# Weight splits moved from GpSimd to VectorE in a routing stage, and the first expert's second weights loaded during it

## The chip, the cores and the metric

One core of one Trainium2 chip runs the whole kernel. The time is device microseconds of one execution. The engines are named as in the profile: PE (TensorE, matmuls; its weight loads are PEld), DVE (VectorE), ACT (ScalarE), POOL (GpSimd) and SP (SyncE, which here only issues transfers). Each engine works through its own instructions in order; semaphores hold an instruction until what it needs is there, and everything queued behind it on that engine waits too.

## The reference

Attention over 4 x 12 heads of 448 tokens, then a mixture of 8 experts with a fixed capacity of 224 tokens each, then a two-layer feed-forward net. Cut to what matters:

```python
x = attention(q, k, v)                       # 1792 tokens x 768
logits = x @ w_gate                          # 1792 x 8
for idx in argsort(-logits.flatten()):       # best (token, expert) pair first
    tok, e = idx // 8, idx % 8
    if assigned[tok] < 0 and counts[e] < 224:
        assigned[tok] = e; counts[e] += 1
for e in range(8):
    out[assigned == e] = relu(x[assigned == e] @ w1[e]) @ w2[e]
h = out @ w_in                               # 768 -> 2048
result = elu(h) @ w_out                      # 2048 -> 768
```

## The kernel before

**Stages.** Attention (to about 302 us), routing (to about 336), the experts (to about 590), the two layers of the last net (to the end). Products are made in float16 pairs: each float32 operand becomes a high half (ACT, a rounding copy) and a low half (what is left: operand times scale minus the high half), and a product is three matmuls (high x high, high x low, low x high).

**Routing** (`Route.run`, L562). Attention leaves the logits `L`. A first round and four more (`round_`, L626; `KSTEP` is 5) raise a price per expert: POOL multiplies (`V`, L628), DVE picks each token's best expert (`choose`) and then in `raises` computes `s` (L602), `u` (L606) and a comparison `gd` (L612); PE counts tokens per expert over the 128 partitions (`cnt`, L617 and L619), DVE tests the count (`ind`, L620), PE turns that into the step, DVE applies it to `U` (L634). It is one chain through DVE and PE; PE fills its waits with nine 512-wide matmuls on constants per round (`warm`). `place` (L639) turns the choice into positions (`pre`, on PE), a 0/1 matrix `Pm` and the token index list `idx` (matmuls `ip`). Then POOL gathers the rows of expert 0 (`gather`, L857), and all engines load a flag `fi` and branch over a rare fallback (L700).

**Weights in the routing stage** (`Weights`, L758). Expert 0's `w1` comes in eight blocks of 128x768. Five float32 stage buffers hold them (`fa`); a buffer is free for the next load when its split is done. In each of the first four rounds ACT scales a block in place (`W.scale`, L773) and later makes its high half (`W.high`, L779), and POOL makes the low half in the next round (`W.low`, L785). The last four blocks get high halves behind the last round and low halves on DVE behind the branch (L926).

**Experts** (`moe`). `columns(e)` splits the gathered rows (`xg`) into halves `xh` (high on ACT L896; low on DVE for expert 0, on POOL L897 for the others) and transposes them on PE (`xt`, L904). The first products (`ph`, L940, 8 of 18 matmuls, three PSUM banks) end in a ReLU on ACT (L941) and a low half on DVE (L944), which together free the bank. The second products (`py`, L956) are 6 of 24 matmuls. `W.split` (L791, L800, L802) loads and splits the weights of all later experts; SP issues the loads. What stands inside `tc.manual_schedule()` is written in the order in which it is to be issued; everything else is placed by a scheduler that models time, and it may place its instructions between those of a manual block. The list `idx` is also stored to memory element by element (`lin`, L929, on ACT's queue) and read back on SP's (`id2`, L931) for the last scatter.

Of the kernel before, what the change touches and what calls it, by code (L numbers as in the profile page):

```python
# [504 lines left out]
class Route:  # L505
# [54 lines left out]
    def run(self, L, idx, row_d, W, gather):  # L560
# [9 lines left out]
        with tc.tile_pool(name="rt", bufs=1, reuse_waits="tile") as sp, \  # L570
# [55 lines left out]
            def round_(n, Lc, r, *beside):  # L626

                nc.gpsimd.tensor_tensor(V, U, bc(r), ALU.mult)  # L628
                W.low()
# [6 lines left out]
                if beside:  # L636
                    W.high()

            def place():  # L639
# [13 lines left out]
                Pm, Q = T("Pm", [P, 112, NT], F16), T("Qm", [P, NT, 2, 8], F16)  # L653
                nc.gpsimd.tensor_tensor(Q[:, :, 0], oh, self.tok.unsqueeze(2).broadcast_to(tile3), ALU.mult)
# [13 lines left out]
                nc.vector.tensor_copy(fi, f)  # L668

# [16 lines left out]
            with tc.manual_schedule():  # L686
                for h in H:
                    nc.vector.tensor_tensor(U[:, h], L[:, h], bc(self.t0, h.stop - h.start), ALU.subtract)
                warm(8)
                round_(0, L, self.iw, W.scale, relative)  # L690
                for k in range(1, KSTEP):
                    round_(1, Ln, self.r, *(W.scale,) * (k < KSTEP - 1))
                for k in range(4, 8):
                    W.high(False)
                choose(Ln)
                fi = place()
                gather()
                warm(3)
# [59 lines left out]
class Weights:  # L758

    def __init__(self, tc, ring, w1_d):  # L760
        self.tc, self.nc, self.wstage, self.ring = tc, tc.nc, ring, ring
        self.w1_d, self.fs, self.ws, self.todo = w1_d, [], [], None
# [7 lines left out]
    def scale(self):  # L770

        f = self.fs[len(self.ws)]
        self.nc.scalar.activation(f, f, AF.Copy, scale=SW)  # L773

    def high(self, scaled=True):
# [3 lines left out]
        self.nc.scalar.activation(w[:, 0], f, AF.Copy, scale=1.0 if scaled else SW)  # L779
        self.todo = f, w  # L780

    def low(self):
        if self.todo:
            f, w = self.todo
            self.nc.gpsimd.tensor_tensor(w[:, 1], f, w[:, 0], ALU.subtract)  # L785
            self.todo = None
            self.load()
# [6 lines left out]
    def split(self, tag, bufs, src, n, name, f=None):  # L794
        nc = self.nc
        if f is None:
            f = self.stage(src, n, name)
# [63 lines left out]
def moe(tc, xs, idx, idh, W, rows, ring, w1_d, w2_d, wi_d, wo_d, lin, g_d, t_d, out):  # L861
    nc = tc.nc
    with tc.tile_pool(name="xc", bufs=1, reuse_waits="tile") as xp, tc.tile_pool(name="mp", bufs=1, space=PSUM, reuse_waits="tile") as pp:
# [19 lines left out]
        with tc.tile_pool(name="m1", bufs=1, reuse_waits="tile") as sp:  # L883
# [34 lines left out]
            with tc.manual_schedule():  # L918
# [4 lines left out]

                nc.vector.tensor_copy(ix2[0:112], idx[0:112])
                for f in range(4, 8):
                    nc.vector.scalar_tensor_tensor(W.ws[f][:, 1], W.fs[f], SW, W.ws[f][:, 0], ALU.mult, ALU.subtract)  # L926
                W.after = columns(0)
# [3 lines left out]
            nc.sync.dma_start(id2, lin.rearrange("(g p) -> p g", p=P))  # L931
            for e in range(E):
                x = xe[e]
                h = sp.tile([P, 8, 2, CAP], F16, tag="h", name=f"h{e}", bufs=2)
                for f in range(8):
                    w = W.ws[f] if e == 0 else W.split("w1", 8, w1_d[e, f], 768, f"w1_{e}_{f}")
# [5 lines left out]
                    if e == 0 and f == 3:  # L942
                        W.after = relu.ins
                    nc.vector.scalar_tensor_tensor(h[:, f, 1], ps, 0.0, h[:, f, 0], ALU.max, ALU.subtract)  # L944
# [6 lines left out]
                for d in range(6):  # L951
                    w = W.split("w2", 6, w2_d[e, d], 1024, f"w2_{e}_{d}", W.fs[8 + d] if e == 0 and d < 4 else None)
# [4 lines left out]
                    result(e, d, ps)  # L957
        with tc.tile_pool(name="wb", bufs=1, reuse_waits="tile") as wp:
# [176 lines left out]
```

## Time and profile before

| | |
|---|---|
| Median of three runs | 1012.69 us (1010.31 to 1017.13) |
| Profiled execution | 1012.46 us, of it span 1010.7 |
| PE busy | 956.9 us, 95% |
| DVE busy | 757.9 us, 75% |
| ACT busy | 525.1 us, 52% |
| POOL busy | 292.6 us, 29% |
| Chain that ended last | PE 54%, DMA 8%, DVE 2% |

A row of a timeline has the start in us, the length in us, the engine, the line, the operation, what it writes and reads, and how many instructions were merged (x18); in brackets the engine's idle time before it and what ended that. A row of a group by line has the busy sum and the mean of one, then the idle time before the group and who ended it. In a row of a tile are the shortest, median and longest duration in ns. The chain of waits is the path that ended last, in order of time.

### The profile page before, as it was taken

The numbers are of one execution on the slowest core, as the hardware profiler recorded it, in microseconds if no ns is written. First come the engines' busy times: TensorE is split into PE (matmuls) and PEld (weight loads), VectorE is DVE, ScalarE is ACT, GpSimd is POOL, SyncE is SP. The second block draws the span as 40 slices with busy tenths as digits, with TensorE's granted clock in tenths as the row PEclk, the third lists the DMA queues.
The fourth block names the chain that finished last, engine by engine and source line by source line (L and its number), as shares of the span: only waits on it lengthen the run. The fifth ranks groups of instructions, "written<-read, shape, count | busy, mean of one in ns | idle before, by whom it ended". The sixth has DMA issues, their size and how long they took to land.

```text
span 1010.7 us, 18583 instructions
## 1 busy us (share of the span) xinstructions
PE 956.9 (95%) x6922; PEld 630.2 (62%) x6922; DVE 757.9 (75%) x1412; ACT 525.1 (52%) x1152; POOL 292.6 (29%) x438
## 2 busy tenths in 40 slices
PE   5899999999997878999999999999999989999997
PEld 2445555555554568999999965555555546666664
DVE  7899999999958458877778699999933574555530
ACT  4778888888864256666664443343411333332330
POOL 5678888888623530221100000000000001000000
PEclk7999999999998889999999999999999999999999
DMA  9434344344221589977777258788784653333100
GB/s 343 150 104 127 118 116 147 114 126 138 51 52 53 82 248 313 289 252 231 219 235 218 80 185 275 248 261 273 216 260 123 191 156 100 109 116 101 46 32 32
DMA packets 100639, 164.92 MB, mean 163 GB/s; under 512 B 32960, under 2 KB 66240, under 8 KB 100160
## 3 DMA queue, kind: packets, MB, share of 16 engines
q1 hardware_dynamic: 95760, 150.56, 47.4%
q0 software_dynamic: 2400, 11.01, 3.3%
q10 hardware_dynamic: 2384, 2.10, 1.3%
q8 instruction: 56, 0.92, 0.4%
q14 instruction: 39, 0.32, 0.1%
HBM read 131.66 MB, written 31.99 MB: 162 GB/s over the span
## 4 chain that ended last, share of the span: by engine, by line
PE 54%; DMA 8%; DVE 2%; issue 1%; ACT 0%; SPq 0%; POOL 0%; POOLq 0%; ACTq 0%; DVEq 0%
PE l L1034 17%; PE py L956 10%; PE o_b L1073 10%; PE ph L940 9%; PE o_c L1073 6%; DMA g_d<-e 3%; PE o_a L1073 2%; DMA fw<-w 2%; DMA xg<-xs,idx 1%; DMA q<-g_d 1%; PE xt L904 1%; DVE e L1038 0%; DMA out<-xc,id 0%; DVE w L802 0%; DVE e L1037 0%
## 5 line engine op out<-in xcount | busy, mean ns | idle before, releaser
L1034 PE MATMUL l<-xc,wic 128*128 128x384 f16 (+1 forms) x1152 | 218.2, 352 | 0.0
L1034 PEld LDWEIGHTS <-wic 128*128 128x128 f16 x1152 | 112.7, 98 | 104.8
L1073 PEld LDWEIGHTS <-a 128*128 128x128 f16 x1080 | 106.1, 98 | 75.2 <-ACT a L1010 3.5
L1089 POOL DMA_INDIRECT out<-xc,id x14 | 14.4, 1030 | 468.8 <-DVE xc L1082 443.1
L802 DVE SCALAR_TENSOR_TENSOR w<-fw,w 128x768 f16<-128x768 f32 (+1 forms) x100 | 114.9, 1154 | 27.9 <-ACT w L800 27.6
L244 ACT ACTIVATE p<-s,nb,r 128x448 f32<-128x448 f32 x144 | 103.9, 722 | 31.2 <-DVE nb L231 30.9
L956 PE MATMUL py<-h,w 128*128 128x224 f16 x1152 | 113.8, 259 | 2.0 <-ACT h L941 1.2
L956 PEld LDWEIGHTS <-w 128*128 128x128 f16 x1152 | 109.9, 98 | 2.6 <-issue 2.3
L225 DVE TENSOR_REDUCE nm<-s 128x1 f32<-128x448 f32 x168 | 102.9, 613 | 3.5 <-PE s L220 3.1
L940 PE MATMUL ph<-xe,w 128*128 128x224 f16 x1008 | 99.5, 259 | 2.5 <-DVE h L944 2.5
L800 ACT ACTIVATE w<-fw 128x768 f16<-128x768 f32 (+1 forms) x100 | 92.9, 932 | 15.2 <-DMA fw<-w 14.6
L940 PEld LDWEIGHTS <-w 128*128 128x128 f16 x1008 | 96.4, 98 | 3.1 <-issue 2.8
L1036 ACT ACTIVATE e<-l 128x512 f32<-128x512 f32 (+1 forms) x64 | 34.6, 540 | 113.0 <-PE l L1034 112.7
L297 PE MATMUL o<-e,v 128*64 128x448 f32 x384 | 87.8, 558 | 1.6 <-DVE xl L309 1.6
L282 ACT ACTIVATE e<-pt 128x448 f32<-128x448 f32 (+2 forms) x216 | 82.8, 422 | 12.3 <-PE pt L273 11.2
L273 PE MATMUL pt<-idn,p 128*128 128x128 f32 x432 | 71.2, 277 | 2.0 <-ACT p L244 1.5
L273 PEld LDWEIGHTS pt<-idn,p 128*128 128x128 f32 x432 | 50.4, 141 | 24.3 <-ACT e L282 16.7
L897 POOL TENSOR_TENSOR xh<-xg,xh 112x768 f16<-112x768 f32 x14 | 25.0, 1802 | 137.8 <-ACT xh L896 137.8
L220 PE MATMUL s<-ks,qh 128*128 128x448 f16 x144 | 52.0, 361 | 12.5 <-ACT p L244 10.8
L231 DVE TENSOR_TENSOR nb<-nm,r 128x1 f32<-128x1 f32 x168 | 59.4, 354 | 2.9
L1010 ACT ACTIVATE a<-s 128x1024 f16<-128x1024 f32 (+2 forms) x30 | 28.5, 966 | 55.4 <-PE o_b L1073 31.9
L1073 PE MATMUL o_b<-wb,a 128*128 128x384 f16 x312 | 52.7, 326 | 0.0
(246 smaller groups left out, 1653.8 us busy)
## 6 DMA issues: line engine op xcount, KB each, us to landing
fw<-w SPq DMA_DIRECT2D x44, 512.0 KB, 4.8
fw<-w SPq DMA_DIRECT2D x56, 384.0 KB, 3.9
xwi<-wi SPq DMA_DIRECT2D x16, 768.0 KB, 6.6
xwo<-wo SPq DMA_DIRECT2D x16, 768.0 KB, 4.9
q<-g_d SPq DMA_DIRECT2D x24, 512.0 KB, 3.7
qT<-qT SPq DMA_DIRECT2D x24, 448.0 KB, 4.1
qk<-qk SPq DMA_DIRECT2D x23, 448.0 KB, 3.4
g_d<-e SPq DMA_DIRECT2D x32, 256.0 KB, 4.4
```

The costliest lines, as they stand in the source:

```text
L225: nc.vector.tensor_reduce(d["nm", u], d["s", u][:, 0:448], AX.X, ALU.max, negate=True)
L231: nc.vector.tensor_tensor(d["nb", u], d["nm", u], d["r"][:, rc:rc + 1], ALU.mult)
L244: nc.scalar.activation(dst, d["s", u][:, 0:448], AF.Exp, bias=d["nb", u], scale=d["r"][:, rc:rc + 1], accum_out=d["sm"][:, rc:rc + 1])
L273: nc.tensor.transpose(pt[:, j * P:(j + 1) * P], p[j][:, h, 64 * h + c * P:64 * h + (c + 1) * P], idn)
L282: move = nc.vector.tensor_copy if u not in (0, 1, 2, 4, 5, 6) else lambda o, x: nc.scalar.activation(o, x, AF.Copy)
L297: nc.tensor.matmul(d["o"][64 * h:64 * h + 64, 0:448], d["v"][:, c + 4 * h, :], d["e", min(2 * c + h, 6)], start=c == 0, stop=c == 3)
L800: nc.scalar.activation(w[:, 0], f, AF.Copy, scale=SW)
L802: nc.vector.scalar_tensor_tensor(w[:, 1], f, SW, w[:, 0], ALU.mult, ALU.subtract)
L940: nc.tensor.matmul(ps, w[:, i, d * P:(d + 1) * P], x[:, d, j], start=d == 0 and n == 0, stop=d == 5 and n == 2)
L956: nc.tensor.matmul(ps, w[:, i, f * P:(f + 1) * P], h[:, f, j], start=f == 0 and n == 0, stop=f == 7 and n == 2)
L1034: nc.tensor.matmul(ps, w[:, i, d * P:(d + 1) * P], xc[cb][:, h, d, j], start=d == 0 and m == 0, stop=d == 5 and m == 2)
L1073: nc.tensor.matmul(ps, a[x][:, f, i], wt[b][f][:, j], start=first and f == 0 and k == 0, stop=f == 7 and k == 2, skip_group_check=True)
```

## The change

POOL makes no low halves any more. `W.scale` is gone: `W.high` makes the scaled high half inside `raises`, where `W.scale` stood, and `W.low` makes the low half on DVE in pieces of 384 columns: one piece in each of rounds 1 to 4 behind `gd`, two in `place` ahead of the product with `pre`, four ahead of the index list, six behind expert 0's gather. A pool for six blocks of `w2` (512 KB each) is opened before routing and loaded on SP's queue (`W.fetch`); two of their high halves are made behind the last round (`W.second`). Expert 0's first products stand inside the manual block, with the other halves of its `w2` between them (`W.second`, `W.rest`). The four `w2` loads that ACT issued before are gone. `idx` is copied for the store behind `columns(0)`.

```diff
             def round_(n, Lc, r, *beside):
                 nc.gpsimd.tensor_tensor(V, U, bc(r), ALU.mult)
-                W.low()
                 choose(Lc)
                 ...
-                if beside:
-                    W.high()
-            def place():
+            def place(first=lambda: None, second=lambda: None):
                 ...
+                first()
                 nc.gpsimd.tensor_tensor(Q[:, :, 0], oh, ...)
                 ...
                 nc.vector.tensor_copy(fi, f)
+                second()
                 ...
-                round_(0, L, self.iw, W.scale, relative)
+                round_(0, L, self.iw, W.high, relative)
                 for k in range(1, KSTEP):
-                    round_(1, Ln, self.r, *(W.scale,) * (k < KSTEP - 1))
-                for k in range(4, 8):
-                    W.high(False)
+                    round_(1, Ln, self.r, W.high, W.low)
                 choose(Ln)
-                fi = place()
+                fi = place(lambda: W.low(2), lambda: W.low(4))
                 gather()
+                W.second(2)
+                for k in range(3):
+                    W.high()
+                    W.low(2)
...
-    def low(self):
-        if self.todo:
-            f, w = self.todo
-            self.nc.gpsimd.tensor_tensor(w[:, 1], f, w[:, 0], ALU.subtract)
+    def low(self, n=1):
+        for _ in range(n):
+            k, h = divmod(self.halves, 2)
+            self.halves += 1
+            f, w, c = self.fs[k], self.ws[k], slice(384 * h, 384 * h + 384)
+            self.nc.vector.scalar_tensor_tensor(w[:, 1, c], f[:, c], SW, w[:, 0, c], ALU.mult, ALU.subtract)
+            if h:
+                self.load()
+    def fetch(self, pool, w2_d):
+        self.f2 = [pool.tile([P, 1024], F32, name=f"b{d}") for d in range(6)]
+        self.w2 = []
+        for f, x in zip(self.f2, w2_d[0]):
+            self.nc.sync.dma_start(f, x)
+    def second(self, n=1):
+        for _ in range(n):
+            d = len(self.w2)
+            w = self.ring.tile([P, 2, 1024], F16, tag="w2", name=f"w2_0_{d}", bufs=6)
+            self.w2.append(w)
+            self.nc.scalar.activation(w[:, 0], self.f2[d], AF.Copy, scale=SW)
+    def rest(self, d):
+        w = self.w2[d]
+        self.nc.vector.scalar_tensor_tensor(w[:, 1], self.f2[d], SW, w[:, 0], ALU.mult, ALU.subtract)
...
-                nc.vector.tensor_copy(ix2[0:112], idx[0:112])
-                for f in range(4, 8):
-                    nc.vector.scalar_tensor_tensor(W.ws[f][:, 1], W.fs[f], SW, W.ws[f][:, 0], ALU.mult, ALU.subtract)
                 W.after = columns(0)
+                nc.vector.tensor_copy(ix2[0:112], idx[0:112])
                 nc.scalar.dma_start(lin.rearrange("(h e r) -> r (h e)", h=2, e=E), ...)
-                W.fs += [W.stage(w2_d[0, d], 1024, f"b{d}", nc.scalar) for d in range(4)]
+                for f in range(8):
+                    relu = first(0, f, W.ws[f])
+                    if f == 3:
+                        W.after = relu.ins
+                    if f < 6:
+                        if f >= 2:
+                            W.second()
+                        W.rest(f)
             nc.sync.dma_start(id2, lin.rearrange("(g p) -> p g", p=P))
```

What this makes of the engines' orders, at the places that matter below. On DVE, in a routing round, from the comparison to the step; before:

```order
L612 TENSOR_TENSOR gd<-u,GG 128x128x4
L612 TENSOR_TENSOR gd<-u,GG 128x128x8
L620 TENSOR_SCALAR ind<-cnt,c_72 128x8
L634 TENSOR_TENSOR U<-V,k 128x48
L634 TENSOR_TENSOR U<-V,k 128x64
```

and after the change:

```order
L612 TENSOR_TENSOR gd<-u,GG 128x128x4
L612 TENSOR_TENSOR gd<-u,GG 128x128x8
L785 SCALAR_TENSOR_TENSOR wa_5076<-fa_4295,wa_5076 128x384
L620 TENSOR_SCALAR ind<-cnt,c_72 128x8
L633 TENSOR_TENSOR U<-V,k 128x48
L633 TENSOR_TENSOR U<-V,k 128x64
```

One half of a block has come between the comparison and the test that waits for PE's count.

On PE, behind the branch, inside expert 0's product 0 (`ph_0`, weights `wa`; `xt_0` with `xh_1` is a transpose of expert 1's halves); before, where products 0, 1 and 2 have had six matmuls each (`wa_5200` is product 2's weight):

```order
L940 LDWEIGHTS wa_5200
L940 MATMUL ph_2_6782<-xe_6683,wa_5200 128x224
L904 LDWEIGHTS xh_1_6914
L904 MATMUL xt_0_6919<-idh,xh_1_6914 128x112
L904 LDWEIGHTS xh_1_6914
L904 MATMUL xt_0_6919<-idh,xh_1_6914 128x112
L940 LDWEIGHTS wa_5086
L940 MATMUL ph_0_6740<-xe_6683,wa_5086 128x224
```

and after, where only product 0 has had six:

```order
L951 LDWEIGHTS wa_5076
L951 MATMUL ph_0_6752<-xe_6704,wa_5076 128x224
L922 LDWEIGHTS xh_1_6942
L922 MATMUL xt_0_6947<-idh,xh_1_6942 128x112
L922 LDWEIGHTS xh_1_6942
L922 MATMUL xt_0_6947<-idh,xh_1_6942 128x112
L951 LDWEIGHTS wa_5076
L951 MATMUL ph_0_6752<-xe_6704,wa_5076 128x224
```

Expert 1's transposes stand twelve matmuls earlier; the second of them needs the low half from POOL.

On ACT, behind the high halves of expert 0's columns (`xh` with `xg` of the two later experts, `lin` the index store, `fb` the `w2` loads, `h` the ReLUs, `w_1_5` a `w1` block of expert 1); before:

```order
L929 DMA lin<-ix_6646 112x16x1
L791 DMA fb_6729<-w 128x1024
L791 DMA fb_6731<-w 128x1024
L791 DMA fb_6733<-w 128x1024
L896 ACTIVATE xh_1_6914<-xg_1_6656 112x768
L791 DMA fb_6735<-w 128x1024
L896 ACTIVATE xh_0_6913<-xg_0_6655 112x768
L896 ACTIVATE xh_1_7348<-xg_1_6909 112x768
L941 ACTIVATE h_6739<-ph_0_6740 128x224
```

and after, the same place and, further on, that of the last ReLU:

```order
L914 ACTIVATE xh_1_6942<-xg_1_6682 112x768
L914 ACTIVATE xh_0_6941<-xg_0_6681 112x768
L914 ACTIVATE xh_1_7354<-xg_1_6937 112x768
L944 DMA lin<-ix_6672 112x16x1
L952 ACTIVATE h_6751<-ph_0_6752 128x224
...
L952 ACTIVATE h_6751<-ph_6_6892 128x224
L818 ACTIVATE w_1_5_7272<-fw_1_5_7270 128x768
L818 ACTIVATE w_1_6_7298<-fw_1_6_7296 128x768
L952 ACTIVATE h_6751<-ph_7_6913 128x224
```

The index store has gone behind the third gathered half, and two blocks of expert 1 stand ahead of the last ReLU. On SP the six `w2` loads stand behind attention's last stores, then the last three `w1` blocks, then (behind the flag's load, ahead of the branch) the first two `w1` blocks of expert 1; behind the branch three more, `id2`, and only then `w1` blocks 5 to 7.

## Rows read from the trace of the kernel before

**Rows 1.** Chain of waits, from 387 us (start, length, what)
```profile
387.36 0.45 PE ph L940 x3
...
447.23 13.80 PE ph L940 x144
```

**Rows 2.** Timeline of PE, expert 0's first products
```profile
345.41 1.89 PE L940 MATMUL ph<-xe,wa 128*128 128x224 f16 x18
...
359.13 8.89 PE L940 MATMUL ph<-xe,wa 128*128 128x224 f16 x72 [5.85 <-DVE h L944]
```

**Rows 3.** PE's groups by line, 342 to 388 us
```profile
L940 PE MATMUL ph<-xe,wa 128*128 128x224 f16 x144 | 16.2, 278 | 5.9 <-DVE h L944 5.9
L956 PE MATMUL py<-h,w 128*128 128x224 f16 x76 | 8.1, 259 | 2.0 <-ACT h L941 1.2 <-DVE h L944 0.8
L940 PE MATMUL ph<-xe,w 128*128 128x224 f16 x57 | 6.1, 259 | 2.3 <-DVE h L944 2.3
```

**Rows 4.** Timeline of ACT, high halves of gathered rows, first ReLUs
```profile
350.14 0.84 ACT L896 ACTIVATE xh<-xg 112x768 f16<-112x768 f32 x1 [4.96 <-DMA xg<-xs,idx]
357.56 0.84 ACT L896 ACTIVATE xh<-xg 112x768 f16<-112x768 f32 x1 [6.58 <-DMA xg<-xs,idx]
358.31 0.83 ACT L941 ACTIVATE h<-ph 128x224 f16<-128x224 f32 x3
```

**Rows 5.** Tile xg (gathered rows), 330 to 382 us
```profile
DMA to landing us min/median/max: 3.8/8.4/15.9
```

**Rows 6.** Timeline of DVE in routing, rounds 0, 1 and 2
```profile
303.47 0.34 DVE L602 SCALAR_TENSOR_TENSOR s<-V,oh 128x48 f32<-128x48 f32 x2
...
307.42 1.72 DVE L602 SCALAR_TENSOR_TENSOR s<-V,oh 128x48 f32<-128x48 f32 x2
...
311.11 0.23 DVE L620 TENSOR_SCALAR ind<-cnt,c 128x8 f16<-128x8 f32 x1 [0.74 <-PE cnt L619]
...
312.72 1.79 DVE L602 SCALAR_TENSOR_TENSOR s<-V,oh 128x48 f32<-128x48 f32 x2
```

**Rows 7.** Tile fa (w1 stage buffers), 300 to 392 us
```profile
L785 POOL TENSOR_TENSOR wa<-fa,wa x4: 1637/1639/1691, 307.2 to 323.4; 128x768 f16<-128x768 f32 x4
...
DMA to landing us min/median/max: 3.0/3.1/3.1
```

**Rows 8.** Timeline of DVE, the operation of the halves at two widths
```profile
237.64 0.62 DVE L309 SCALAR_TENSOR_TENSOR xl<-o,xh 128x448 f16<-128x448 f32 x1
...
402.11 0.38 DVE L944 SCALAR_TENSOR_TENSOR h<-ph,h 128x224 f16<-128x224 f32 x1
```

**Rows 9.** Stretch table (us, PE busy, granted clock, DMA share, GB/s)
```profile
302.00:328.00 26.00, 20.67 (x141) 0.87 0.19 56
...
388.00:420.00 32.00, 31.75 (x343) 1.00 0.92 308
```

**Rows 10.** Timeline of DVE, from place() to expert 0's columns
```profile
329.95 0.34 DVE L656 TENSOR_TENSOR r<-oh,pre 128x48 f32<-128x48 f16 x2 [1.08 <-PE pre L649]
...
334.71 0.17 DVE L673 TENSOR_SCALAR idx<-ip 112x8 int32<-112x8 f32 x1 [2.11 <-PE ip L671]
...
339.13 0.17 DVE L924 COPY ix<-idx 112x16 int32<-112x16 int32 x1 [3.85 <-DVEq L700]
339.24 3.56 DVE L926 SCALAR_TENSOR_TENSOR wa<-fa,wa 128x768 f16<-128x768 f32 x4
```

**Rows 11.** Timeline of POOL, gathers behind the branch and the next half
```profile
339.20 0.93 POOL L857 DMA_INDIRECT xg<-xs,idx  x1 [1.63 <-DVEq L700]
340.44 1.44 POOL L857 DMA_INDIRECT xg<-xs,idx  x1 [0.30 <-DVE wa L926]
...
345.27 1.64 POOL L897 TENSOR_TENSOR xh<-xg,xh 112x768 f16<-112x768 f32 x1 [0.31 <-ACT xh L896]
```

**Rows 12.** Tile lin (the index store)
```profile
DMA to landing us min/median/max: 10.3/10.3/10.3
```

**Rows 13.** Tile fw (weight loads on SP's queue), 300 to 392 us
```profile
DMA to landing us min/median/max: 3.2/6.0/17.2
```

More of the change, by code (lines that the diff above doesn't have):

```diff
@@ L858, in gather, with moe @@
         return x
-def moe(tc, xs, idx, idh, W, rows, ring, w1_d, w2_d, wi_d, wo_d, lin, g_d, t_d, out):
+def moe(tc, xp, pre, xs, idx, idh, W, rows, ring, w1_d, w2_d, wi_d, wo_d, lin, g_d, t_d, out):
     nc = tc.nc
-    with tc.tile_pool(name="xc", bufs=1, reuse_waits="tile") as xp, tc.tile_pool(name="mp", bufs=1, space=PSUM, reuse_waits="tile") as pp:
+    with tc.tile_pool(name="mp", bufs=1, space=PSUM, reuse_waits="tile") as pp:
         bank = lambda t, name: pp.tile([P, 512], F32, tag=PS[t][0], name=name, bufs=PS[t][1])
@@ L922, in moe, with first @@
                     nc.tensor.matmul(warm, idh, W.ws[0].rearrange("p a b -> p (a b)")[:, 0:512], start=True, stop=True)
+                W.after = columns(0)
                 nc.vector.tensor_copy(ix2[0:112], idx[0:112])
-                for f in range(4, 8):
-                    nc.vector.scalar_tensor_tensor(W.ws[f][:, 1], W.fs[f], SW, W.ws[f][:, 0], ALU.mult, ALU.subtract)
-                W.after = columns(0)
                 nc.scalar.dma_start(lin.rearrange("(h e r) -> r (h e)", h=2, e=E), ix2[0:112].rearrange("p h e -> p (h e)"))
-                W.fs += [W.stage(w2_d[0, d], 1024, f"b{d}", nc.scalar) for d in range(4)]
[L931 to L936, printed above, removed]
+                def first(e, f, w):
+                    x, h = xe[e], hs[e]
                     ps = bank(1, f"ph{e}_{f}")[:, 0:CAP]
@@ L941, in moe @@
                     relu = nc.scalar.activation(h[:, f, 0], ps, AF.Relu)
[L942 to L944 removed]
+                    nc.vector.scalar_tensor_tensor(h[:, f, 1], ps, 0.0, h[:, f, 0], ALU.max, ALU.subtract)
+                    return relu
+                hs = {0: sp.tile([P, 8, 2, CAP], F16, tag="h", name="h0", bufs=2)}
+                for f in range(8):
+                    relu = first(0, f, W.ws[f])
+                    if f == 3:
+                        W.after = relu.ins
+                    if f < 6:
+                        if f >= 2:
+                            W.second()
+                        W.rest(f)
+            nc.sync.dma_start(id2, lin.rearrange("(g p) -> p g", p=P))
+            for e in range(E):
+                if e:
+                    hs[e] = sp.tile([P, 8, 2, CAP], F16, tag="h", name=f"h{e}", bufs=2)
+                    for f in range(8):
+                        first(e, f, W.split("w1", 8, w1_d[e, f], 768, f"w1_{e}_{f}"))
+                h = hs[e]
                 if e + 2 < E:
@@ L1116, in body @@
         rows = Rows(tc, ring, xs, idx)
-        rt.run(L, idx, row, W, rows.gather)
-        moe(tc, xs, idx, idh, W, rows, ring, i["w1"], i["w2"], i["wi"], i["wo"], lin, g_d, t_d, out)
+        with tc.tile_pool(name="xc", bufs=1, reuse_waits="tile") as xp:
+            pre = ExitStack()
+            W.fetch(pre.enter_context(tc.tile_pool(name="pre", bufs=1, reuse_waits="tile")), i["w2"])
+            rt.run(L, idx, row, W, rows.gather)
+            moe(tc, xp, pre, xs, idx, idh, W, rows, ring, i["w1"], i["w2"], i["wi"], i["wo"], lin, g_d, t_d, out)
 def kernel(q, k, v, g_q, g_k, moe_w_gate, moe_w1, moe_w2, moe2_w_in, moe2_w_out):
```

20 lines of the change are left out of this document (7 added, 13 removed).

## Prediction

> **What bounds the kernel now.** The page's table of busy time comes first: PE 95% of the span, so what can be won is where PE stands still or is kept from starting. The chain of waits shows where: from 387.36 us on it is PE work, expert after expert, and a full set of an expert's first products takes 13.80 us for 144 matmuls, 0.0958 us each [rows 1]. Ahead of 387.36 the chain runs through DMA, POOL, ACT and DVE. PE begins expert 0's first products at 345.41 us and resumes at 359.13 after 5.85 us of idling [rows 2]. PE's groups for 342 to 388 us show where it idles: 5.9 us in expert 0's first products, 2.0 in the second, 2.3 in expert 1's first, and always for ACT or DVE [rows 3].
>
> What that stretch costs: from 345.41 to 387.36 are 41.95 us. By the order PE issues in it 270 matmuls (144 and 72 of expert 0, 54 of expert 1) and 25 transposes: 270 x 0.0958 = 25.9 us, and about 1.3 us. The loss is 14.8 us: idling, and 72 matmuls that take 8.89 us instead of 6.9 behind the longest wait [rows 2]. Routing ahead of it is a serial chain in which PE mostly warms itself: what is cut there is cut from the end. From the last first-layer product of expert 2 on, the order of the instructions on PE is that of before, and on the other engines from about there, so later stages should shift whole.
>
> **Why PE stands.** ACT puts three gathered halves (expert 1's two, the first of expert 2) ahead of the first ReLU: it waits 4.96 us for the second, 6.58 us for the third, and only at 358.31 frees the PSUM banks [rows 4]. Landing of the gathers ranges from 3.8 to 15.9 us [rows 5]; in the same microseconds ACT queues the 4-byte store of the index list and 2 MB of w2.
>
> **The change, part by part.** All clock times below are on before's clock; routing's saving comes off at the end.
>
> *Splits off POOL.* In the four rounds that hold a split on POOL, the two VectorE operations `s` (L602) take 1.72 us once and 1.79 us three times; in the round without one they take 0.34 [rows 6]. The split itself lasts 1.64 us [rows 7] and covers just them. From `s` to `s` the round without is 303.47 to 307.42, 3.95 us, the next 5.30. Saving: 1.38 + 3 x 1.45 = 5.7 us. The halves that VectorE takes over (128x384, not in the trace) lie between its 224-wide form, 0.38 us, and its 448-wide form, 0.62 [rows 8]: linear between, 0.55. The cover is VectorE's wait for the count, 0.74 us [rows 6]; without it each would cost 0.55, four 2.2. ACT's scaling in place (0.83 us) goes and the copy takes its place: nothing. The nine warm-up products ran at a granted clock of 0.87 on average in routing [rows 9]. A shorter round keeps PE busier, so I take the full 2.4 GHz; sets at 1.2 GHz would make the count wait for them, which is part of a rival below.
>
> *In place().* Two halves stand in a wait of 1.08 us and four in one of 2.11 [rows 10]: 1.1 and 2.2 by my estimate, 0.1 us over. Bounds: 0, and 0.8 if POOL's product in the first wait also holds them up.
>
> The Trainium skill (SBUF — State Buffer, "Who interferes with whom") says that VectorE with two SBUF inputs and a GpSimd instruction that reads SBUF exclude each other for a whole instruction. The trace agrees: 1.72 to 1.79 against 0.34. It speaks against this change where POOL's masked product meets the first two halves: by it the sum would be about 0.4 us smaller. The page also says that only GpSimd's reads are caught, so descriptor writing for a gather should not slow; the row beside VectorE's splits, 1.44 us against 0.93 [rows 11], says it does, and by the row the gathers cost up to 0.5 us each, by the rule nothing.
>
> *At the branch.* Four halves (2.2 us) now stand before VectorE's branch, which takes 3.85 us behind the index [rows 10]. It runs about 1.9 us later (it is fetched while the last half still runs), and POOL's gather of expert 1, which waited for that branch [rows 11], with it. Behind the branch are two halves (1.1) instead of four whole splits (3.56): VectorE reaches expert 0's columns about 0.5 us earlier. The 18 warm-ups ahead of the transposes limit this; I take 0.4 (from -0.6, if the gathers slow, to 1).
>
> *Expert 0's products.* The order, not the diff, decides: PE still has expert 1's transposes inside product 0, now after six matmuls, before after eighteen. The second needs POOL's lower half, which stands behind four gathers: begun at 339.20, the half at 345.27, 1.64 us long [rows 11]. Shifted by 1.9 it ends at 348.8, and PE, there at 345.0 + 0.6, waits 3.2 us. Then 48 matmuls, 4.6 us: product 3 starts at 353.4 instead of 359.13. ACT holds the ReLUs behind expert 2's gather again. That is issued 3 us after the first, at 344.1; the index store and the w2 loads no longer lie before it, three w1 loads (1.2 MB) beside it do. Between 3.8 and 15.9 I take 6, nearer the bottom because most of that traffic is gone: landed 350.1, ReLU 0 at 351.0. It binds only if landing takes over 7.6 us; at 15.4, the 357.56 of before, it adds 7.8.
>
> *w2 early.* Six 512 KB loads behind the last attention stores fall into a stretch whose DMA share is 0.19 [rows 9] and need to be there only for the copies behind the last round, more than 20 us later. Cost nothing; the cover would fail only past that. The three w1 loads queued behind them on SP land in 3.1 us [rows 7].
>
> *The price of the new order.* ACT now stores the index list behind expert 2's half, at 351.0. SP loads it back (`id2`) when the store has landed, 10.3 us in before [rows 12], at 361.3; the loads of expert 1's w1 rows 5 to 7 stand behind that. ACT has rows 5 and 6 ahead of ReLU 7. PE reaches the first product that needs ReLU 7 after 148 matmuls and 17 transposes, at 368.5. A load behind `id2` took 17.2 us in before, with 2 MB on the other queue; 3.1 is the row without traffic [rows 7, 13]. I take the median of the group, 6.0: row 5 lands at 367.7 (0.4 for the issue), row 6 1.3 later (384 KB at the 308 GB/s that the next stretch moves [rows 9]), ACT's copy of it and the ReLU end at 370.2. PE waits 1.7 us; 0 with 3.1, 13 with 17.2.
>
> **Sum.** Loss in the stretch 3.2 + 1.7 = 4.9 instead of 14.8: 9.9 won. With 5.7 - 0.1 and 0.4: 15.9. The profiled execution took 1012.46 us (span 1010.7), 0.2 below the median of three, 1012.69. 1012.5 - 15.9 = 996.6 us.
>
> **Rivals.**
> - *Everything fits*: the gathers come in sooner and ReLU 7 is there; loss 2 us. Routing 6, start 1, stretch 12.8: 993. For it: the DMA queues are empty at the start. Against: VectorE's branch comes later by the order.
> - *The gathers stay slow*: expert 2's lands after 15 us as before, product 3 at 361: 996.6 + 7.8 = 1004.4. For it: the same three halves stand before the ReLUs. Against: 2 MB less traffic.
> - *Routing saves nothing*: the halves overrun the count by 0.55 each or PE falls to 1.2 GHz in two rounds, and the lock moves to place(): 996.6 + 5.7 = 1002.3. Against: the 0.74 us wait.
> - *Loads behind the index list*: row 5 of w1 lands after 17.2 us as in before, PE waits 13 instead of 1.7: 1008. For it: the order of SP's queue is the same. Against: no 2 MB on the other queue.
> - *Slower*: the same queue, if reading the list back costs another 10.3 us like storing it: 27.5 us, PE waits 23, 1018. It ends above 1012.5 from a wait of 17.6 us on, a landing 22 us behind `id2`. Against: before's 17.2 already holds that read, and 2 MB besides.
>
> **How the numbers follow.** Forecast 0.58, everything fits 0.15, slow gathers 0.07, routing saves nothing 0.08, loads behind the list 0.08, slower 0.04. About 1% is what a measurement of this kernel can tell from no change, 1002.6 to 1022.8. Faster: 0.58 + 0.15 + 0.05 of the routing case (it ends at the edge) + 0.02 of the milder ends of the two transfer cases = 0.80; slower: 0.04, the last case; same: the rest, 0.16. The range: 990 (everything fits, with the lower bounds of all costs) to 1004 leaves out the two late-load cases and half of the slow gathers.
>
> **What would show it.** Rounds of 3.9 to 4.0 us from `s` to `s`, with the 384-wide split inside the wait for the count: right. L602 above 0.34 or a wait for the count that ends on the split: wrong. PE's first product at about 339.3 on the new clock, a wait of some 3 us on POOL's half inside product 0, product 3 about 8 us behind the first. A wait of PE on ReLU 7 of 0 to 4 us; over 8 us means the loads behind the list. All later stages as long as before; if the first layer or the second is longer, the shift was not whole and the forecast is wrong.

## The result, and the profile after

The changed kernel takes 1001.0 us (median of four runs, 1000.04 to 1002.41) where the kernel before took 1012.27 beside it: ratio 0.9883, 95% interval 0.9845 to 0.9920. Run again later beside variants it gave 0.9868 (0.9846 to 0.9890). 996.6 was forecast, with a range of 990 to 1004: faster by over 1%, inside the range, 4.4 us above the point.

| | before | after |
|---|---|---|
| Profiled execution, its span | 1012.46, 1010.7 us | 1000.04, 998.1 us |
| PE / DVE busy | 956.9 / 757.9 us | 953.1 / 754.9 us |
| ACT / POOL busy | 525.1 / 292.6 us | 522.3 / 287.1 us |
| Chain that ended last | PE 54%, DMA 8%, DVE 2% | PE 58%, DMA 5%, DVE 1% |
| Index list begins (DVE `idx`) | 334.71 | 329.02: 5.69 earlier |
| PE's first product of expert 0 | 345.41 | 338.86: 6.55 earlier |
| Start of expert 3's first products on the chain | 447.23 | 434.70: 12.53 earlier |
| End of span | 1010.7 | 998.1: 12.6 earlier |

So the gain arises in three pieces: 5.7 us in routing, 0.9 from the index list to PE's first product, and 6.0 between that and expert 3. From there on everything has moved as a whole. The chain's row that answers to the last of [rows 1]:

```profile
434.70 13.80 PE ph L951 x144
```

Timeline of VectorE in routing, changed kernel (against [rows 6, 10]; start, length, engine, line, operation, count, and in brackets the idle time before it and its releaser): `s` takes 0.34 us beside a round's half, rounds are 3.93 us from `s` to `s`, and 0.27 us of waiting for the count is left behind the half of 0.55.

```profile
307.45 0.34 DVE L602 SCALAR_TENSOR_TENSOR s<-V,oh 128x48 f32<-128x48 f32 x2
...
308.94 0.55 DVE L785 SCALAR_TENSOR_TENSOR wa<-fa,wa 128x384 f16<-128x384 f32 x1
...
309.77 0.23 DVE L620 TENSOR_SCALAR ind<-cnt,c 128x8 f16<-128x8 f32 x1 [0.27 <-PE cnt L619]
...
311.37 0.34 DVE L602 SCALAR_TENSOR_TENSOR s<-V,oh 128x48 f32<-128x48 f32 x2
...
323.10 1.20 DVE L785 SCALAR_TENSOR_TENSOR wa<-fa,wa 128x384 f16<-128x384 f32 x2
...
329.02 0.17 DVE L673 TENSOR_SCALAR idx<-ip 112x8 int32<-112x8 f32 x1 [0.24 <-PE ip L671]
```

Timeline of PE, changed kernel, expert 0's first products (against [rows 2]). The wait that stood behind three products now stands inside product 0, first for ACT's high half of expert 1's rows, then for POOL's low half:

```profile
338.86 0.73 PE L951 MATMUL ph<-xe,wa 128*128 128x224 f16 x6
343.12 0.27 PE L922 MATMUL xt<-idh,xh 112*128 112x112 f16 x1 [3.53 <-ACT xh L914]
344.84 0.27 PE L922 MATMUL xt<-idh,xh 112*128 112x112 f16 x1 [1.44 <-POOL xh L915]
...
346.40 12.70 PE L951 MATMUL ph<-xe,wa 128*128 128x224 f16 x114
```

What is late is the gather. Timelines of POOL and of ACT, changed kernel (against [rows 11] and [rows 4]), and between them a row of its chain of waits: POOL starts expert 1's first gather at 335.06, held by SP's branch, the rows land 7.14 us later, and ACT starts on them at 342.23. In the kernel before the same gather landed 3.84 us after its start (339.20 to 343.04; it is the 3.8 of [rows 5]). Further down in ACT's timeline stands its wait for expert 2's w1 at 379.79, which comes back further on.

```profile
335.06 1.31 POOL L875 DMA_INDIRECT xg<-xs,idx  x1 [2.77 <-SPq L702]
```

```profile
335.06 7.14 DMA xg<-xs,idx
```

```profile
342.23 0.84 ACT L914 ACTIVATE xh<-xg 112x768 f16<-112x768 f32 x1 [4.54 <-DMA xg<-xs,idx]
...
347.76 0.36 ACT L952 ACTIVATE h<-ph 128x224 f16<-128x224 f32 x1 [1.47 <-PE ph L951]
...
379.79 0.84 ACT L818 ACTIVATE w<-fw 128x768 f16<-128x768 f32 x1 [3.51 <-DMA fw<-w]
```

PE by groups and as one stretch, from the first product to expert 3's first products (stretch table: from:to, length, PE busy, granted clock, DMA share, GB/s). First the changed kernel, then the kernel before: PE's idle time in it is 6.4 us after, 12.1 before, its busy time the same.

```profile
L951 PE MATMUL ph<-xe,w 128*128 128x224 f16 x290 | 28.8, 259 | 1.4 <-DVE h L953 1.4
L951 PE MATMUL ph<-xe,wa 128*128 128x224 f16 x144 | 16.6, 280 | 0.0
L922 PE MATMUL xt<-idh,xh 112*128 112x112 f16 x75 | 5.8, 219 | 5.0 <-ACT xh L914 3.5 <-POOL xh L915 1.4
...
338.80:434.70 95.90, 89.48 (x941) 0.96 0.78 231
```

```profile
L904 PE MATMUL xt<-idh,xh 112*128 112x112 f16 x73 | 5.6, 213 | 1.7 <-POOL xh L897 1.5 <-ACT xh L896 0.2
...
345.40:447.20 101.80, 89.71 (x939) 0.97 0.87 259
```

The same table in stretches, changed kernel. In the first two, w1 loads of expert 1 run beside the gathers (before: 118 GB/s from 334 to 340); in the third PE mostly waits, and the granted clock of the third and the fourth is 0.61 and 0.54, so mostly 1.2 GHz; in the fifth the DMA engines move little, 72 GB/s, though their busy share is 0.67, and in the sixth 273.

```profile
334.00:340.00 6.00, 5.59 (x43) 0.83 0.80 254
340.00:346.00 6.00, 1.44 (x8) 0.74 0.82 219
...
342.00:346.00 4.00, 1.44 (x8) 0.61 0.67 184
346.00:350.00 4.00, 4.00 (x27) 0.54 0.76 54
...
346.00:357.00 11.00, 11.00 (x100) 0.83 0.67 72
357.00:380.00 23.00, 23.00 (x251) 1.00 0.87 273
```

### The profile page after: what moved, and what is told of

It reads as the page before. It is cut to its first block, busy times and chain, and to the rows that moved or that the text cites. A ratio compares the mean times of both kernels' runs of the same rounds, so it can differ in the third digit from the quotient of the medians.

```text
span 998.1 us, 18586 instructions
## 1 busy us (share of the span) xinstructions
PE 953.1 (95%) x6922; PEld 629.7 (63%) x6922; DVE 754.9 (76%) x1424; ACT 522.3 (52%) x1148; POOL 287.1 (29%) x434
## 4 chain that ended last, share of the span: by engine, by line
PE 58%; DMA 5%; DVE 1%; issue 1%; SPq 0%; ACT 0%; POOL 0%; POOLq 0%; ACTq 0%; DVEq 0%
PE l L1062 17%; PE ph L951 11%; PE py L983 11%; PE o_b L1101 10%; PE o_c L1101 6%; DMA g_d<-e 3%; PE o_a L1101 2%; PE xt L922 1%; DMA q<-g_d 1%; DMA xg<-xs,idx 1%; DVE e L1066 0%; DMA out<-xc,id 0%; DVE e L1065 0%; SPq L1022 0%; POOL xh L915 0%
## 5 line engine op out<-in xcount | busy, mean ns | idle before, releaser
L820 DVE SCALAR_TENSOR_TENSOR w<-fw,w 128x768 f16<-128x768 f32 (+1 forms) x98 | 110.0, 1127 | 25.9 <-ACT w L818 25.8
L818 ACT ACTIVATE w<-fw 128x768 f16<-128x768 f32 (+1 forms) x98 | 90.6, 928 | 5.9 <-DMA fw<-w 5.6
L220 PE MATMUL s<-ks,qh 128*128 128x448 f16 x144 | 52.0, 361 | 12.5 <-ACT p L244 10.8
L1039 DVE SCALAR_TENSOR_TENSOR a<-s,a 128x1024 f16<-128x1024 f32 (+2 forms) x30 | 33.1, 1117 | 26.1 <-ACT a L1038 26.0
```

Of the source, the lines that this page charges most:

```text
L818: nc.scalar.activation(w[:, 0], f, AF.Copy, scale=SW)
L820: nc.vector.scalar_tensor_tensor(w[:, 1], f, SW, w[:, 0], ALU.mult, ALU.subtract)
```

## The experiments

Ratios are to the kernel before, run beside each group of four; there it took 1014.0 to 1014.7 us, so 0.001 is 1 us.

| kernel | median us | ratio (95%) |
|---|---|---|
| changed kernel, first / again | 1001.0 / 1001.73 | 0.9883 (0.9845 to 0.9920) / 0.9868 (0.9846 to 0.9890) |
| e1 routing alone | 1008.61 | 0.9949 (0.9931 to 0.9966) |
| e2 no early w2 | 1009.10 | 0.9950 (0.9933 to 0.9966) |
| e3 no hand order | 1001.21 | 0.9875 (0.9856 to 0.9893) |
| e4 transposes late | 997.01 | 0.9827 (0.9808 to 0.9847) |
| e5 list back late | 1000.43 | 0.9868 (0.9846 to 0.9889) |
| e6 = e5, two w1 loads late | 1002.40 | 0.9895 (0.9872 to 0.9918) |
| e7 = e4 + e5 | 996.11 | 0.9830 (0.9806 to 0.9855) |
| e8 two halves a round | 999.36 | 0.9861 (0.9837 to 0.9885) |
| e10 = e5, more stage buffers | 1002.28 | 0.9878 (0.9857 to 0.9898) |
| e11 = e7, more stage buffers | 1001.08 | 0.9868 (0.9848 to 0.9889) |
| e12 = e7 + e8 | 996.59 | 0.9824 (0.9806 to 0.9843) |

(e9 is the changed kernel again.)

### Which part won what: e1, e2, e3

**e1**, only the routing part; the first products stand outside the manual block and w2 goes through `W.split`, as before:

```diff
-            W.fetch(pre.enter_context(...), i["w2"])
...
-                W.second(2)
...
+                W.fs += [W.stage(w2_d[0, d], 1024, f"b{d}", nc.scalar) for d in range(4)]
...
```

> Routing as in the changed kernel (low halves on VectorE, POOL makes none), the experts as before: expert 0's w2 loaded by ACT behind the index store, its first products placed by the scheduler, expert 1's transposes after eighteen matmuls. Theory (the routing term stands alone, 5.7 us): four rounds of 3.9 to 4.0 us, L602 at 0.34 us, the first product about 6 us earlier, and everything behind shifted whole: 1012.3 - 5.7 = 1006.6 us, at most 1 us to either side. Rival (the two parts of the change depend on each other, and earlier routing is eaten by the wait for the gathers): 1009 us or more. Rival (the routing saving is larger than what shows, and the new order of the experts gave some back): 1003 us or less.

5.2 us faster (3.4 to 7.0). In its trace L602 is 0.34 in all rounds, rounds are 3.93 us, the index list begins at 329.28: the routing term stands. The experts are as before: ACT stands for the second and third gathered half ahead of the first ReLU, and PE resumes at 355.30. Timelines of ACT and PE in e1:

```profile
349.11 0.84 ACT L914 ACTIVATE xh<-xg 112x768 f16<-112x768 f32 x1 [6.74 <-DMA xg<-xs,idx]
353.74 0.84 ACT L914 ACTIVATE xh<-xg 112x768 f16<-112x768 f32 x1 [3.79 <-DMA xg<-xs,idx]
```

```profile
355.30 9.89 PE L952 MATMUL ph<-xe,wa 128*128 128x224 f16 x72 [3.06 <-DVE h L954]
```

**e2**, the early load undone, the hand order kept:

```diff
-            W.fetch(pre.enter_context(...), i["w2"])
...
                 nc.scalar.dma_start(lin...)
+                W.fs += [W.stage(w2_d[0, d], 1024, f"b{d}", nc.scalar) for d in range(4)]
...
-                    if f < 6:
-                        if f >= 2:
-                            W.second()
-                        W.rest(f)
...
```

> The changed kernel without the early load of expert 0's w2: four blocks are loaded on ACT's queue behind the index store and two on SP's, and split where they are used; routing and the first products issued by hand stay. Theory (the early load took the w2 copies and their landing out from ahead of the ReLUs): the copies of w2 wait for their loads on ACT ahead of ReLU 4, PE stands 3 us or more between products 3 and 7 of expert 0 or in its second products, 1004 to 1007 us. Rival (the loads are hidden anyway, all of the gain in the experts is the hand-written order): 1001 us, within 1 us.

Routing's gain and no more; without the early load the hand order wins nothing. PE's wait inside product 0 is only 2.5 us here, since no w1 load could go ahead of the branch (the stage buffers are wanted for w2) and the gather landed in 3.9 us (335.89 to 339.78). But ACT then waits for w2 three times ahead of ReLU 4 (4.80, 0.67 and 3.79 us), which comes only at 364.07, and PE stands 4.42 us in the second products. Timelines of ACT and PE in e2:

```profile
339.78 0.84 ACT L914 ACTIVATE xh<-xg 112x768 f16<-112x768 f32 x1 [2.65 <-DMA xg<-xs,idx]
...
356.54 1.06 ACT L818 ACTIVATE w<-fb 128x1024 f16<-128x1024 f32 x1 [4.80 <-DMA fb<-w]
...
363.11 1.06 ACT L818 ACTIVATE w<-fb 128x1024 f16<-128x1024 f32 x1 [3.79 <-DMA fb<-w]
```

```profile
364.46 0.53 PE L980 MATMUL py<-h,w 128*128 128x224 f16 x2 [4.42 <-ACT h L953]
```

**e3**, the hand order undone (the first products stand in the loop over experts again), the early load kept:

```diff
-                for f in range(8):
-                    relu = first(0, f, W.ws[f])
...
+                for f in range(2, 6):
+                    W.second()
+                for f in range(6):
+                    W.rest(f)
...
```

> The changed kernel with expert 0's first products placed by the scheduler again (routing and the early w2 load stay). On PE expert 1's transposes then stand after eighteen matmuls, as before; on ACT four copies of w2 stand ahead of ReLU 0. Theory (the wait for expert 1's halves is the same wherever its transposes stand, and product 3 waits for the copies about as long as it now waits for the order): product 3 at about 351 to 352 us, 1001 us within 1.5 us, so the hand-written order by itself gives nothing. Rival (the hand-written order is what won the 6 us): 1004 us or more.

The time of the changed kernel. Four w2 copies stand ahead of ReLU 0 (3.88 us from 347.75) and product 3 starts at 354.94, later than expected, but later waits are shorter. So of the experts' 6 us the early load carries all, the hand order nothing that can be measured. By e1 to e3 the two gains add up: 5.2 from routing, and 0.0066 to 0.0082 in ratio (e1 or e2 against the changed kernel, both its runs), 7 to 8 us, from the load.

What the load removes depends on the order. Under the scheduler's order it is the late gathers: the second gather of expert 1 and the first of expert 2 landed after 11.9 and 15.3 us in e1, after 7.5 and 9.3 in e3. Under the hand order it is ACT's waiting for w2 (e2). One rival is left: e1 and e2 put w2 back not only later but behind the index store on ACT's queue, where its blocks took 12 to 21 us to land. No run loads it late on another queue, so what the time of the load and what its queue is worth are not told apart.

### The wait inside product 0: e4, e6, e8

**e4**, expert 1's halves behind ReLU 2, its transposes behind product 7 (`columns` makes the halves and returns a function that issues the transposes):

```diff
                         W.rest(f)
+                    if f == 2:
+                        turn1 = columns(1)
+                turn1()
```

> The changed kernel with expert 1's halves made behind ReLU 2 and its transposes issued behind expert 0's product 7 instead of inside product 0. Theory (PE's 5.0 us of waiting inside product 0 for expert 1's gathered rows, and the 1.6 us that the matmuls behind it lose at the granted clock of 0.5, are there only because of where the transposes stand): PE has no wait inside product 0, products 0 to 5 take 0.096 us a matmul, 1001.0 - 6.6 = 994.4 us, 993 to 997. Rival (the time comes back a few us later, as a wait for expert 1's w1 blocks, for the ReLUs behind their copies, or for expert 1's transposes): 998 to 1002 us.

Faster than the changed kernel: 0.9827, against 0.9868 and 0.9883, 4 to 6 us by the medians' ratios. The intervals just touch, but no single time does: 997.8 at most, against 1000.0 at least. Products 0 to 5 run through; the wait was there because of where the transposes stood. Part of it comes back, as the rival said, in two waits. The first, 1.52 us ahead of product 7, is not one for ReLU 6: product 7 needs the PSUM bank of product 4, and VectorE's low half of ReLU 4, which frees it, stands behind four splits of expert 1's w1 (350.93, 5.00 us). The second, 2.84 us, is for ReLU 7, which on ACT stands behind blocks 5 and 6 of expert 1's w1; SP had stood 15.3 us for the index store with these loads behind it. Timelines of PE and VectorE and table of waits of SP (engine, line, releaser: sum, times, longest) in e4:

```profile
338.80 10.51 PE L954 MATMUL ph<-xe,wa 128*128 128x224 f16 x108
...
356.29 1.89 PE L954 MATMUL ph<-xe,wa 128*128 128x224 f16 x18 [1.52 <-DVE h L956]
...
363.73 0.83 PE L989 MATMUL py<-h,w 128*128 128x224 f16 x7 [2.84 <-ACT h L955]
```

```profile
350.93 5.00 DVE L820 SCALAR_TENSOR_TENSOR w<-fw,w 128x768 f16<-128x768 f32 x4
355.86 0.38 DVE L956 SCALAR_TENSOR_TENSOR h<-ph,h 128x224 f16<-128x224 f32 x1
```

```profile
SPq L971 <- DMA lin<-ix: 15.3, 1, 15.3
```

**e6** is e5 (below) and:

```diff
                 nc.scalar.dma_start(lin...)
+                pre1 = [W.stage(w1_d[1, f], 768, f"w1_1_{f}", nc.scalar) for f in range(2)]
...
+                        first(e, f, W.split(..., pre1.pop(0) if pre1 else None))
...
```

> The kernel of e5_list_back_late, with the first two w1 blocks of expert 1 loaded on ACT's queue behind the index store, so that SP has no load between the flag and the branch. Theory (the gathers of the changed kernel land late, 7.1 us for expert 1's first, because these loads share the DMA engines with them): the first gather lands in about 4 us, PE stands about 2.5 us inside product 0 instead of 5.0 and its matmuls behind that run at the full clock: 997 to 998.5 us. Rival (the gathers are slow whatever runs beside them, or are held by the branch alone): 5 us of waiting again, at most 0.5 us better than e5_list_back_late. Rival (the blocks now come too late for expert 1): a wait of PE for them, no gain or a loss.

The edit did only part of what it was meant to: the first two blocks are late, but SP now issues the third, at 330.60, ahead of the branch. The gather lands in 5.85 us instead of 7.1, starts 1.2 us sooner (two of VectorE's halves fell behind the branch in this order), and PE stands 2.0 us inside product 0: that much as expected. The median is no better than e5's, and even in the profiled execution (999.42, the fastest of six that reach 1005.28) most of it is gone again: PE waits 3.00 us for VectorE behind w1 of expert 2 and resumes at 385.10, against 386.13 in e5. Timeline of PE in e6:

```profile
340.64 0.22 PE L922 MATMUL xt<-idh,xh 112*128 112x112 f16 x1 [0.51 <-ACT xh L914]
342.36 0.22 PE L922 MATMUL xt<-idh,xh 112*128 112x112 f16 x1 [1.49 <-POOL xh L915]
...
385.10 5.34 PE L952 MATMUL ph<-xe,w 128*128 128x224 f16 x54 [3.00 <-DVE h L954]
```

The landing of this gather goes with what runs beside it from 334 to 340 us: 3.8 us at 118 GB/s (before), 3.9 at 116 (e2), 5.5 at 190 (e3), 5.7 at 199 (e1), 7.1 at 254 (changed kernel), 7.6 at 250 (e5), 7.0 at 263 (e8); e6, at 266, has 5.85. This fits loads that share the DMA engines with the gather and cost it up to 3 us, but it is a comparison of kernels that differ in more than these loads. e6 and e8 both issue three w1 loads between 328 and 337 us, where the changed kernel issues five, and lie over 1 us apart, so the price is not settled.

**e8**, two halves in each round, none ahead of the index list:

```diff
-                    round_(1, Ln, self.r, W.high, W.low)
+                    round_(1, Ln, self.r, W.high, lambda: W.low(2))
...
-                fi = place(lambda: W.low(2), lambda: W.low(4))
+                fi = place(lambda: W.low(2))
```

> The changed kernel with two low halves on VectorE in each of rounds 1 to 4 instead of one, and none ahead of the index list. Theory (the cover of the halves is VectorE's wait for the count; 0.27 us of it is left behind one half): the second half, 0.55 us, overruns it by 0.28 us a round, 3.93 becomes 4.2 us, 1.1 us slower than the changed kernel: 1002.1 us. Rival (a half costs nothing there, PE's count is later anyway): 1001.0 us. Rival (the halves cost their whole length): rounds of 4.5 us, 1003.2 us.

The wait for the count is used up, and the second half costs 0.10 us a round, rounds of 4.03, not 0.28. In time no difference that can be told. VectorE in e8:

```profile
307.45 0.35 DVE L602 SCALAR_TENSOR_TENSOR s<-V,oh 128x48 f32<-128x48 f32 x2
...
308.95 1.02 DVE L785 SCALAR_TENSOR_TENSOR wa<-fa,wa 128x384 f16<-128x384 f32 x2
309.88 0.22 DVE L620 TENSOR_SCALAR ind<-cnt,c 128x8 f16<-128x8 f32 x1
...
311.48 0.34 DVE L602 SCALAR_TENSOR_TENSOR s<-V,oh 128x48 f32<-128x48 f32 x2
```

This order too has two halves fewer ahead of the branch: POOL's gather starts 5.10 us behind `idx` instead of 6.04. That is about half a microsecond for each half, as the prediction said; but with the same four halves ahead the distance ranges from 5.64 us (e3) to 6.40 (e9).

### The loads behind the index list: e5, e7, e10, e11, e12

**e5** puts the loading back of the index list behind expert 3's w1 loads on SP; **e7** is that edit and e4's together:

```diff
-            nc.sync.dma_start(id2, lin...)
...
+                if e == 3:
+                    with tc.issue_after(W.last.ins):
+                        nc.sync.dma_start(id2, lin...)
```

> The changed kernel with only the loading back of the index list moved: it stands on SP behind expert 3's w1 loads instead of ahead of rows 5 to 7 of expert 1's w1, where SP stood 20.7 us for the index store. Theory (the term that the prediction put at 1.7 us is real but small: PE never waited for ReLU 7 in the changed kernel): ACT's two waits for rows 5 and 6, 0.77 and 0.58 us, go, PE gains nothing there and at most the 1.45 us at 385.7: 999.5 to 1001. Rival (the queue behind the list costs more than the trace shows, through all later loads): 998 us or less.

> The kernel of e4_turn_late (expert 1's transposes behind product 7) with the loading back of the index list behind expert 3's w1 loads. In e4_turn_late SP stood 15.3 us for the index store, the DMA engines were nearly idle from 346 to 354 us (busy share 0.11), and PE stood 1.52 and 2.84 us for ReLU 6 and ReLU 7 behind rows 5 and 6 of expert 1's w1. Theory (the queue behind the list is that wait): both waits go, 4 us better than e4_turn_late. Rival (row 5 needs the stage buffer of row 0, which is split only at 350 to 352 us, so the load could start 1.4 us earlier and no more): 1 to 1.5 us better.

e5 is the changed kernel's time; ACT still waits 1.35 us for row 5 (w1 block 5 of expert 1), which needs the buffer of row 0, split at 355 us. In **e7** PE's wait for ReLU 7 and its low half falls from 2.84 to 0.51 us. The wait ahead of product 7 stays (1.43): as in e4 it is for the low half of ReLU 4 behind VectorE's four splits, which has nothing to do with the list, so the theory could not have both waits go. Its profile is 2 us shorter than e4's, its median 0.9, with intervals that overlap: the queue behind the list is a cause of the wait, what it is worth is not settled.

**e10** and **e11** load w2 of experts 1 to 7 into the six buffers of the early load:

```diff
-        f = self.stage(src, n, name)
+        if d is None:
+            f = self.stage(src, n, name)
+        else:
+            f = self.f2[d]
+            self.last = nc.sync.dma_start(f, src)
```

> The kernel of e5_list_back_late, with the w2 blocks of experts 1 to 7 loaded into the six buffers that hold expert 0's early w2, as soon as those are split, instead of into the five shared stage buffers. In the changed kernel the DMA engines moved 72 GB/s from 346 to 357 us and 273 GB/s from 357 to 380, and in four kernels whose first products ended between 356 and 359 us PE resumed at 384.8 to 386.1 all the same, behind w1 of expert 2. Theory (the weight stream is the next bound, held back by the stage buffers): four w2 blocks fill the empty stretch, over 150 GB/s from 346 to 357, the wait near 385 goes, 1.5 us better than e5_list_back_late. Rival (the stream is bound by its bytes, and rows 5 to 7 of expert 1's w1, now behind 2 MB, come later): a wait of 2 to 4 us for ReLU 7, 1 to 3 us worse.

> The kernel of e7_turn_late_list_late with the same six buffers for w2 as in e10_more_stage. Theory (the same stream): the waits behind expert 1's second products go, but rows 5 to 7 of its w1 come about 3 us later, so PE stands 3 to 5 us for ReLU 6 and 7: 997 to 999 us. Rival (the buffers alone held the stream): 994 us or less.

The wait at 385 is gone in e10, but the stretch from 346 to 357 us is as empty as before, 53 GB/s (the first w2 load for them goes out at 350.90), and the rival's wait for ReLU 7 is there. In e11 it goes out at 343.08, and the stretch does fill: 185 GB/s where e7 has 37. It still falls back from 996.1 to 1001.1 by one wait of 5.90 us, because rows 5 and 6 of expert 1's w1, issued at 353.69 and 354.56 behind the w2 blocks, land after 10.3 and 11.4 us. So the buffers alone did not help: where they fed the stream sooner, they only changed which block is late. Stretch table and PE in e10, then PE in e11:

```profile
346.00:357.00 11.00, 11.00 (x100) 0.83 0.33 53
...
369.95 1.38 PE L989 MATMUL py<-h,w 128*128 128x224 f16 x8 [2.36 <-ACT h L956]
```

```profile
367.11 2.58 PE L995 MATMUL py<-h,w 128*128 128x224 f16 x13 [5.90 <-ACT h L959]
```

**e9**, the changed kernel again, and **e12**, e7 with e8's rounds:

> The changed kernel itself once more, beside the variants, so that they can be compared on one chip. Every theory expects a ratio near 0.988 to the kernel before; a profile with a wait of about 5 us inside product 0 and one of 1 to 2 us in expert 1's first products near 385 us.

> The kernel of e7_turn_late_list_late with two low halves a round as in e8_two_halves_a_round (rounds of 4.03 instead of 3.93 us there, two halves instead of four ahead of the branch). Theory (with the wait inside product 0 gone the earlier branch brings nothing, and the rounds cost 0.4 us): the time of e7_turn_late_list_late, 995.5 to 997 us. Rival (the earlier branch starts the first products earlier): 994.5 us or less.

e9 agrees (its waits: 4.8 us inside product 0, 2.71 near 385). e12 is e7's time. e4, e7 and e12 beat both kernels: 996 to 997 us, about 17.5 us below the kernel before.

## Why the prediction was right or wrong

**Routing, 5.7 us: right, in mechanism and size.** 5.69 in the trace, 5.2 by e1. The half took the 0.55 us that was interpolated from two widths, and stood in the wait for the count. The fall-back price ("without it each would cost 0.55") was not put to the test: e8's second half adds 0.47 us (two in a row take 1.02), finds 0.27 of the wait left, and costs 0.10 a round.

**In place(), 0.1 us: right, nothing was lost.** The two halves took 1.20 us there and 1.02 in e8's rounds, and POOL's product beside them 0.62 where the same shape later took 0.38. The Trainium skill (SBUF — State Buffer, "Who interferes with whom") says that such a pair exclude each other; the trace agrees in that both get longer, by about 0.2 us each, where the prediction read 0.4 out of the rule.

**At the branch: the right size, but more than one engine holds it.** The gather of expert 1 starts 1.55 us later than routing's shift alone would put it (1.9 forecast). The profile names SP's branch in the changed kernel, e7, e9 and e10, VectorE's in e3 to e6, e8, e11 and e12: they end within a few tenths, VectorE idling about 3 us at its own. The Trainium skill (Runtime: NRT & Kernel Launch, "Instruction fetch mechanics") says that a taken branch to code outside the fetched window waits for a DMA fetch; the traces show the waits at the branch (3.05 us on VectorE in the changed kernel), not what they consist of. Whether VectorE's splits slow the issue of a gather stays open: expert 0's second gather took 1.33 us in the changed kernel and 0.93 in e9, in the same place.

**The first product, 0.4 us: right** (6.55 earlier in all; 6.0 forecast).

**Expert 0's products, 3.2 us of wait: the place was right, the size wrong.** It is 4.97. The step that failed moved before's row of POOL's low half by the branch's delay alone, and so kept before's landing. In before nobody on the path was waiting for that gather: it landed at 343.04, 3.84 us after its start, and ACT, held by VectorE, reached its rows only at 344.34, so ACT's row showed no wait for it. In the new order it lands 7.14 us after its start, beside w1 loads of expert 1, the first two of which SP now issues ahead of the branch. That stood in the order shown with the change, and the sum left it out. With no w1 load beside it, it lands in 3.9 (e2). That these loads are what delays it is argued, not shown: e6 moves two of them and the landing falls from 7.6 (e5) to 5.85, but its branch comes earlier too, and e8 with as many loads as e6 has 7.0.

**The clock behind that wait: missing from the sum.** The loss of 14.8 us before counted 72 slow matmuls as 2.0 us to be won; but the 120 matmuls behind the new wait (6 and 114) take 13.6 us on the chain instead of 11.5, at a granted clock of 0.61 from 342 to 346 us and 0.54 from 346 to 350. The wait that was moved took its slow stretch along: 2.1 us. With the longer wait and this stretch product 3 starts about 13 us behind the first and not 8 (ReLU 2, which waits for product 2, starts at 352.24). Not every wait does this: in e8, behind 2.2 us of waiting, the granted clock stayed at 1.00 and 114 matmuls took 11.1 us, while in e2, behind 2.5, it was 0.63 from 342 to 346.

**ReLU 0 not held by expert 2's rows: right.** It waits for PE at 347.76.

**w2 early "costs nothing": right, and undervalued.** The prediction put the gain down to the new order and to 2 MB less beside the gathers. e2 and e3 show that the load, taken from behind the index store, is the whole gain of the experts, and that the order by itself is worth nothing. The 2 MB less are borne out under the scheduler's order (e1 against e3); under the hand order the load removes a wait that the prediction did not name, ACT's for w2 ahead of ReLU 4 (4.80 and 3.79 us in e2).

**ReLU 7, 1.7 us: not seen, though the mechanism is there.** The longer wait inside product 0 covered it; e4, which takes that away, has it with 2.84 us, and e7 cuts it to 0.51.

**Not foreseen: 1.45 us in expert 1's first products** (1.72 in e5, 2.71 in e9), behind w1 of expert 2. In the changed kernel, e5, e6, e8 and e9 products 0 to 6 of expert 0 end between 356 and 359.2 us, and all five resume here between 384.8 and 386.6; in the changed kernel ACT waits for the w1 load until 379.79, and from there on ACT and VectorE work without a gap up to PE's release. So the weights' arrival seems to decide, more than when PE was ready; no run moves it alone. What would feed them sooner is open; e10 and e11 show that more buffers alone don't.

The terms make up most of the difference: 15.9 - 1.8 (longer wait) - 2.1 (clock) - 1.45 (w1 of expert 2) + 1.7 (ReLU 7) + 0.55 (start) = 12.8, against 12.5. The 14.8 itself, a length less an estimate of the work, was about 0.9 too large: idling in that stretch adds up to 11.9 with the transposes' 1.7, and with 2.0 of slow matmuls to 13.9. With that the sum gives 11.9, so the account closes to 0.6 us. Some luck is in the forecast: the 1.7 and 0.55 that went the other way hid part of what was missing.

"All later stages as long as before" held: from expert 3's first products to the end the shift is 12.5 to 12.6 us.

## What to carry to other kernels

Before a wait of the old trace is moved to a new place, ask whether anybody waited for the transfer behind it; if not, read the landing of the transfer itself, and ask what the change newly issues beside it. A wait on TensorE that moves can take its slow stretch at the lower clock along, so that stretch belongs on both sides of the sum. And when splits wait on ACT ahead of the operation that frees a PSUM bank, bringing their loads forward into an idle DMA stretch was here worth more (7 to 8 us) than any order of the products that was tried (0, and 4 to 6 in e4).

## What the runs showed of the hardware that was not expected

A 7 KB store of single 4-byte elements took 11.7 us to land (345.53 to 357.26; 9.7 in e2, 11.8 in e4). The read behind it held SP's whole queue for longer, 20.7 us (24.4 in e2, 15.3 in e4), because it stood in the queue before the store was issued. The store by itself does not keep the DMA engines busy: in e4 it was on its way from 339.92 to 351.71, and from 346 to 350 us their busy share was 0.11, at 4 GB/s. And a gather of 112 rows landed in 3.8 to 7.7 us (before, e4), with traffic of 118 and 256 GB/s beside it.
